# A new order of loads and work at the start of an attention and gMLP block, and six weight loads moved by three blocks

## The chip, the cores and the metric

The kernel runs on one core of one Trainium2 chip. The metric is the device time in microseconds (us) of one execution. Before the change the median was 1889.34 us in 4 runs (1888.5 to 1889.51).

## The reference

```python
mod = (silu(c) @ w_mod).reshape(1, 6, 1, 1024)       # sa, ca, ga, sb, cb, gb
h = layernorm(x) * (1 + ca) + sa                     # x: 2048 rows of 1024
x = x + ga * A(h)      # A: q = h @ wq; 32 heads of 128 against given K and V
                       #    (2048 keys each), softmax, then @ wo
h = layernorm(x) * (1 + cb) + sb
x = x + gb * B(h)      # B: gMLP, 1792 + 1792 columns, 2048 x 2048 spatial product
```

All tensors are bf16. The change touches only the first line of work (the layer norm of x, the modulation with ca and sa, the first query product) and the loads of wq.

## The kernel before

Attention runs in 64 "halves": one head against 1024 of the 2048 queries. Each half has 16 "blocks" kb of 128 keys. A block is two score products ("sps"), one exponential on ACT ("pt"), two output products ("ops"), one DVE addition of the exponentials ("pacc"), and a few products of a later query projection ("qps"), which DVE casts to bf16 ("qT"), as filling. When a half has ended, the sums in pacc go to DRAM and come back transposed ("pT"), DVE reduces them ("den"), and the reciprocals go through DRAM once more ("rec", "rbc"). DVE copies the output products out of PSUM ("ou") and multiplies them by rbc ("oT"). Nearly all loads are issued by one engine, SP, in program order.

```python
    load_wm(nc.scalar, 0, 1)
    load_wm(nc.scalar, 1, 1)
    for j in range(4):                     # SP: x and w_mod interleaved
        for t in range(2):
            nc.sync.dma_start(xg[j][:, t], x_dram[:, 2 * j + t, :])
        load_wm(nc.sync, j, 0)
    ...
    silu()
    for ti in range(9):                    # row tiles 0 to 7 (the first 1024 rows)
        if ti < 8:
            row[ti] = row_stats(xg[ti // 2][:, ti % 2, :])       # DVE
        if ti == 0:
            silu_end()
        else:
            xt = xg[(ti - 1) // 2][:, (ti - 1) % 2, :]
            centre(xt, row.pop(ti - 1), xt)                      # DVE
            if ti % 2 == 0:                # two tiles: turn on PE, copy out on ACT
                ...                        # 16 transposes into hps
                nc.scalar.activation(h1T[...], hps[...], ACT.Copy)
                if j > 0:
                    mod_products(j - 1)    # PE: the columns of ca and sa
                keep_busy(6)               # six dummy matmuls
            elif ti > 3:
                mod_columns(ti // 2 - 2)
    mod_products(3)
    mod_columns(2)
    for j in range(4):                     # h1T = h1T * (1 + ca) + sa
        if j == 3:
            mod_columns(3)
        modulate(2 * j, 0)
        modulate(2 * j + 1, 0, nc.scalar if j else nc.vector)
    keep_busy(8)
    ...
    load_wq(0)                             # 1 MB: the query weights of four heads
    load_kv(0)
    load_wq(1)
    ...
    for g, (i, kb) in enumerate(steps):    # attention: half i, block kb
        ...
        if kb == 2 and i < 16:
            load_kv(halves[i + 1][0])
            if i == 12:
                load_wq(2)
        elif kb == 2 and qh == 0 and h + 1 < H:
            load_kv(h + 1)
            if h % 4 == 2 and h + 2 < H:
                load_wq((h + 2) // 4)
        ...
        if i > 0:
            work = {0: store_sums, 3: turn_sums, 10: finish_den, 13: load_rec}.get(kb)
            if work:
                work(i - 1)
```

The six loads of wq_t inside attention fall into halves 12, 20, 28, 36, 44 and 52.

The softmax here doesn't subtract the row's maximum and nothing guards it: scores larger than these inputs give would overflow.

## Time and profile before

| what | before |
|---|---|
| span of the profiled execution | 1887.7 us |
| PE busy | 1855.4 us (98%) |
| first "pt" of attention (end of the start) | 35.76 us |
| the first 63 of 64 halves of attention, from first pt to first pt | 1119.8 us |
| PE waits for the qT cast ("sps") | 7.7 us, 11 times |

PE is the bound: it is busy 98% of the span and is 90% of the chain. So time can be won only where PE has nothing to do: in the start, and in stalls of attention.

The waits over the whole span (engine and line, what it waited for, us in total, times, longest):

```profile
DVE den L325 <- DMA pT<-sums_dram: 14.9, 8, 3.0
...
PE sps L282 <- DVE qT L266: 7.7, 11, 1.6
...
PE ops L461 <- DVE ou L467: 3.6, 3, 1.7
...
PE qps L262 <- DVE qT L266: 2.6, 3, 1.3
```

Half 12 in the timeline (start, duration, engine, line, what; in brackets the idle time before, and what ended it). A half of this kind takes 17.3 us; this one took 18.98.

```profile
256.19 0.36 SPq L314 DMA_DIRECT2D sums_dram<-pacc  x1
...
256.65 2.16 SPq L244 DMA_TRANSPOSE kT<-in_A_k_cache_dram  x1
...
258.91 0.52 SPq L246 DMA_DIRECT2D v_sb<-in_A_v_cache_dram  x1
...
259.49 1.96 SPq L239 DMA_DIRECT2D wq_t<-in_A_wq_dram  x1
...
261.50 2.74 SPq L318 DMA_TRANSPOSE pT<-sums_dram  x1
...
269.50 1.22 DVE L325 TENSOR_REDUCE den<-pT 128x8 f32<-128x1024 bf16 x1 [2.98 <-DMA pT<-sums_dram]
...
272.43 0.38 PE L282 MATMUL sps<-qT,kT 128*128 128x512 bf16 x1 [1.62 <-DVE qT L266]
```

Read it downwards. The sums are stored at 256.19. Then K, V and 1 MB of wq_t are put into the queue, and only then pT. pT lands at 269.50; DVE has idled 2.98 us for it and, working in order, has left everything behind it undone, also the cast of qT that PE needs. So PE stands 1.62 us.

The start, from the same view:

```profile
18.99 1.28 DVE L126 BATCH_NORM_STATS2 stats<-xg 128x6 f32<-128x512 bf16 x2 [0.17 <-DMA xg<-in_A_x_dram]
...
23.69 1.23 DVE L131 TENSOR_SCALAR xg<-xg,mv,rstd 128x1024 bf16<-128x1024 bf16 x1 [0.31 <-POOL rstd L120]
...
26.53 1.88 ACT L215 ACTIVATE h1T<-hps 128x2048 bf16<-128x2048 bf16 x1 [2.77 <-PE hps L213]
...
28.44 1.92 DVE L195 TENSOR_SCALAR h1T<-h1T,cols 128x1024 bf16<-128x1024 bf16 x4 [0.91 <-ACT h1T L215]
...
30.95 3.62 PE L262 MATMUL qps<-h1T,wq_t 128*128 128x512 bf16 x16
...
34.60 0.69 DVE L266 CAST qT<-qps 128x512 bf16<-128x512 f32 x1 [1.03 <-PE qps L262]
...
35.76 2.85 ACT L450 ACTIVATE pt<-sps 128x1024 bf16<-128x1024 f32 x3 [3.82 <-PE sps L282]
```

The last row tiles of x land at 18.99 (DVE waited 0.17 us), DVE centres the last at 23.69 to 24.92, PE turns it, ACT copies it out of PSUM from 26.53 to 28.41, then DVE and ACT modulate, and the 16 query products run from 30.95. Attention begins with pt at 35.76.

### The profile page before, as it was taken

Reading aid. Unit: us, or ns where it says so; the run is one execution under the profiler, and the core shown is the slowest. Engines: PE = TensorE matmul, PEld = TensorE weight load, DVE = VectorE, ACT = ScalarE, POOL = GpSimd, SP = SyncE. Lnnn points to the kernel's source line nnn. Section 1 sums busy time; section 2 is a strip of 40 time slices with the busy share of each in tenths; the row PEclk is TensorE's granted clock in tenths of the full one; section 3 lists DMA queues with packets and bytes.
Section 4 is the critical chain, followed back from the end, with each engine's and each line's share of the span. In section 5 each row is a group of like instructions: output and inputs, shape, how many; then the busy total and the mean of one; then the engine's idle time right before and its main releaser. Section 6 shows DMA issues by size and latency. Waiting matters only on the chain.

```text
span 1887.7 us, 24331 instructions
## 1 busy us (share of the span) xinstructions
PE 1855.4 (98%) x8873; PEld 851.2 (45%) x8873; DVE 1283.2 (68%) x2131; ACT 1099.4 (58%) x1155; POOL 31.8 (2%) x55
## 2 busy tenths in 40 slices
PE   7999999999999999999999999999999999999999
PEld 3444444444444444444444444444445444444444
DVE  6899888888888888888888888454455400333334
ACT  4888989888888899999999997000013332000000
POOL 1000000000000000000000000000000000000000
PEclk9999999999999999999999999999999999999999
DMA  9585575564555443555565444764214022221102
GB/s 240 146 188 136 135 166 131 128 170 115 140 138 136 116 123 97 151 145 130 150 164 125 114 107 111 191 178 119 66 46 95 6 51 78 52 46 50 45 1 78
DMA packets 396793, 217.35 MB, mean 115 GB/s; under 512 B 297856, under 2 KB 354176, under 8 KB 396672
## 3 DMA queue, kind: packets, MB, share of 16 engines
q1 hardware_dynamic: 392512, 213.70, 44.6%
q10 hardware_dynamic: 4160, 2.10, 0.4%
q8 instruction: 69, 1.13, 0.2%
q14 instruction: 52, 0.43, 0.1%
HBM read 124.26 MB, written 43.52 MB: 89 GB/s over the span
## 4 chain that ended last, share of the span: by engine, by line
PE 90%; DMA 4%; DVE 4%; SPq 1%; issue 1%; ACT 0%; DVEq 0%; ACTq 0%
PE sps L282 20%; PE ops L461 20%; PE acc L372 12%; PE gps L598 10%; PE qps L262 10%; PE zps L548 5%; PE bo L619 5%; PE zps L582 5%; DMA pT<-sums_dram 3%; DVE pacc L471 2%; PE mod_ps L413 1%; DVE den L325 1%; SPq L239 1%; DMA xg<-in_A_x_dram 0%; DVE qT L266 0%
## 5 line engine op out<-in xcount | busy, mean ns | idle before, releaser
L450 ACT ACTIVATE pt<-sps 128x1024 bf16<-128x1024 f32 x1024 | 1017.2, 1025 | 121.2 <-PE sps L282 88.7
L471 DVE TENSOR_TENSOR pacc<-pacc,pt 128x1024 bf16<-128x1024 bf16 x896 | 615.0, 686 | 60.6 <-ACT pt L450 1.3
L282 PE MATMUL sps<-qT,kT 128*128 128x512 bf16 x2048 | 610.7, 379 | 8.5 <-DVE qT L266 7.7
L461 PE MATMUL ops<-pt,v_sb 128*128 128x512 bf16 x2048 | 609.4, 379 | 3.9 <-DVE ou L467 3.6
L262 PE MATMUL qps<-h1T,wq_t 128*128 128x512 bf16 x1024 | 344.3, 379 | 2.6 <-DVE qT L266 2.6
L282 PEld LDWEIGHTS <-kT 128*128 128x128 bf16 x2048 | 200.0, 98 | 253.6 <-issue 16.2
L461 PEld LDWEIGHTS <-v_sb 128*128 128x128 bf16 x2048 | 199.9, 98 | 251.5 <-issue 11.1
L372 PE MATMUL acc<-wo_t,ot 128*128 128x512 bf16 x992 | 216.9, 379 | 0.0
L550 ACT ACTIVATE z<-zps 128x448 bf16<-128x448 f32 x64 | 34.8, 543 | 290.3 <-PE zps L548 287.4
L598 PE MATMUL gps<-wsp,z 128*128 128x512 bf16 x896 | 193.9, 379 | 0.0
L601 DVE TENSOR_TENSOR g<-gps,b_bc 128x512 bf16<-128x512 f32 x56 | 38.7, 692 | 222.1 <-PE gps L598 222.1
L262 PEld LDWEIGHTS <-wq_t 128*128 128x128 bf16 x1024 | 100.1, 98 | 120.9
L372 PEld LDWEIGHTS <-ot 128*128 128x128 bf16 x992 | 96.4, 98 | 113.5
L598 PEld LDWEIGHTS <-z 128*128 128x128 bf16 x896 | 87.7, 98 | 105.7
L266 DVE CAST qT<-qps 128x512 bf16<-128x512 f32 x128 | 88.4, 691 | 41.2 <-PE qps L262 41.0
L548 PE MATMUL zps<-z2w,h2T 128*128 128x448 bf16 x512 | 97.3, 352 | 0.0
L619 PE MATMUL bo<-w_out_t,z1T 128*128 128x512 bf16 x448 | 97.2, 379 | 0.0
L582 PE MATMUL zps<-h2T,z1w 128*128 128x512 bf16 x448 | 96.9, 379 | 0.0
L325 DVE TENSOR_REDUCE den<-pT 128x8 f32<-128x1024 bf16 x63 | 74.8, 1187 | 14.9 <-DMA pT<-sums_dram 14.9
L143 DVE COPY h2T<-hps 128x1024 bf16<-128x1024 bf16 x16 | 11.0, 691 | 97.2 <-PE hps L142 97.2
L346 DVE TENSOR_TENSOR oT<-ou,rbc 128x1024 bf16<-128x1024 f32 x62 | 75.6, 1219 | 0.7 <-DMA rbc<-rec_dram 0.7
L548 PEld LDWEIGHTS <-h2T 128*128 128x128 bf16 x512 | 50.0, 98 | 46.5 <-issue 0.2
(74 smaller groups left out, 695.0 us busy)
## 6 DMA issues: line engine op xcount, KB each, us to landing
rbc<-rec_dram SPq DMA_DIRECT2D x64, 512.0 KB
v_sb<-in_A_v_cache_dram SPq DMA_DIRECT2D x40, 512.0 KB
sums_dram<-pacc SPq DMA_DIRECT2D x63, 256.0 KB
oT_dram<-oT SPq DMA_DIRECT2D x62, 256.0 KB
ot<-oT_dram SPq DMA_DIRECT2D x24, 512.0 KB
wq_t<-in_A_wq_dram SPq DMA_DIRECT2D x8, 1024.0 KB
wm_l<-in_w_mod_dram SPq DMA_DIRECT2D x8, 1024.0 KB
wo_t<-in_A_wo_dram SPq DMA_DIRECT2D x8, 1024.0 KB
```

The source lines that it names most:

```text
L262: nc.tensor.matmul(box["ps"][:], wq_t[:, dc, hc:hc + DH], h1T[:, dc, q0:q0 + 512], start=(dc == 0), stop=(dc == KD - 1))
L266: nc.vector.tensor_copy(out=out_t[:, j * 512:(j + 1) * 512], in_=box["ps"][:])
L282: nc.tensor.matmul(sps[:, j * 512:(j + 1) * 512], kts[h][:, kb * P:(kb + 1) * P], qts[(h, qh)][:, j * 512:(j + 1) * 512], start=True, stop ...
L325: nc.vector.tensor_reduce(out=den[:], in_=state[i]["pT"][:], op=ALU.add, axis=mybir.AxisListType.X)
L372: nc.tensor.matmul(accs[ti][:, sl], lhs, wo_t[:, hh, sl], start=(hh == 0), stop=(hh == H - 1))
L450: nc.scalar.activation(pt[:], s_tiles.pop(g)[:], ACT.Exp, scale=SCALE)
L461: nc.tensor.matmul(o_ps[j][:], vs[h][:, kb, :], pt[:, j * 512:(j + 1) * 512], start=(kb == 0), stop=(kb == NKB - 1))
L471: nc.vector.tensor_add(out=pacc[:], in0=pacc[:], in1=pt[:])
L548: nc.tensor.matmul(zps[:], h2T[:, dc, ti * P:(ti + 1) * P], z2w[:, dc, sl], start=(dc == 0), stop=(dc == KD - 1))
L582: nc.tensor.matmul(zps[:], w[:, dc, :], h2T[:, dc, q * 512:(q + 1) * 512], start=(dc == 0), stop=(dc == KD - 1))
L598: nc.tensor.matmul(gps[:], z2[s][:, f * P:(f + 1) * P], wsps[q][:, s, :], start=(s == 0), stop=(s == NT - 1))
L619: nc.tensor.matmul(bo[:], z1T[:, f, ti * P:(ti + 1) * P], w_out_t[:, f, sl], start=(f == 0), stop=(f == NF - 1))
```

## The change

The intent: shorten the start (load x first; give ACT two of the eight row statistics; modulate the last 256 rows straight out of PSUM, with no copy before; request the first head's wq, K and V early; load the exponential's table first) and keep the 1 MB wq_t loads from standing in front of pT. The dummy matmuls fall from 32 to 10. The core of the diff (helpers and renamings cut):

```diff
+    nc.scalar.activation(small.tile([P, 1], FP32, name="warm_e")[:], eps_tile[:], ACT.Exp)
     load_wm(nc.scalar, 0, 1)
     load_wm(nc.scalar, 1, 1)
-    for j in range(4):
-        for t in range(2):
-            nc.sync.dma_start(xg[j][:, t], x_dram[:, 2 * j + t, :])
-        load_wm(nc.sync, j, 0)
+    for ti in range(8):
+        nc.sync.dma_start(xg[ti // 2][:, ti % 2], x_dram[:, ti, :])
+    load_wm(nc.sync, 0, 0)
+    ...                                   # and 1, 2, 3
+    nc.sync.dma_start(wq_g[0][:, :, 0:256], wq_v[:, :, 0:256])
+    nc.sync.dma_start(out=kts[0][:], in_=A_k_cache[0, 0], transpose=True)
+    nc.sync.dma_start(vs[0][:], A_v_cache[0, 0].rearrange("(kb p) d -> p kb d", p=P))
+    nc.sync.dma_start(wq_g[0][:, :, 256:512], wq_v[:, :, 256:512])
...
+    def stats_act(ti):                    # mean and mean square on ACT
+        ...
+        nc.scalar.activation(junk[:], src, ACT.Identity, scale=1.0 / D, accum_out=mv[:, 0:1])
+        nc.scalar.activation(junk[:], src, ACT.Square, scale=D ** -0.5, accum_out=mv[:, 1:2])
...
-    for ti in range(9): ...
+    dve(0); silu_end(); dve(1); norm(0); stats_act(2); dve(3); norm(1); turn(0)
+    keep_busy(4); mod_products(0); finish_act(2); stats_act(5); dve(4); norm(2); norm(3)
+    turn(1); mod_columns(0); keep_busy(4); dve(6); norm(4); finish_act(5); dve(7); norm(5)
+    turn(2); mod_products(1); mod_products(2); norm(6); norm(7); mod_columns(1)
+    turn(3, False); keep_busy(2); mod_products(3); mod_columns(2)    # tile pair 3 stays in PSUM
+    for dc in range(4):
+        modulate(dc, 0, 768)
+    ...                                   # 768 columns from SBUF, 256 straight from PSUM
...
-    load_wq(0)
-    load_kv(0)
-    load_wq(1)
+    nc.sync.dma_start(wq_g[1][:], wq_v[:, :, 512:1024])
...
-            if i == 12:
-                load_wq(2)
...
-            if h % 4 == 2 and h + 2 < H:
-                load_wq((h + 2) // 4)
...
         if i > 0:
+            if kb == 5 and (i == 12 or i > 16 and qh == 0 and h % 4 == 2 and h + 2 < H):
+                load_wq((h + 2) // 4 if i > 16 else 2)
             work = {0: store_sums, 3: turn_sums, 10: finish_den, 13: load_rec}.get(kb)
```

More of the change, by code (lines that the diff above doesn't have):

```diff
@@ L105, in load_wm @@
         eng.dma_start(wms[j][:, k], wmod_v[:, :, k * D + j * 256:k * D + (j + 1) * 256])
+    wq_v = A_wq.rearrange("(dc p) hd -> p dc hd", p=P)
+    wq_g, kts, vs, qts = {}, {}, {}, {}
+    for g in range(2):
+        wq_g[g] = att.tile([P, KD, 4 * DH], BF16, name="wq_t", tag="wq_t", bufs=2)
+    kts[0] = att.tile([P, S], BF16, name="kT", tag="kT", bufs=2)
+    vs[0] = att.tile([P, NKB, DH], BF16, name="v_sb", tag="v_sb", bufs=2)
+    nc.scalar.activation(small.tile([P, 1], FP32, name="warm_e")[:], eps_tile[:], ACT.Exp)
     load_wm(nc.scalar, 0, 1)
     load_wm(nc.scalar, 1, 1)
-    for j in range(4):
-        for t in range(2):
-            nc.sync.dma_start(xg[j][:, t], x_dram[:, 2 * j + t, :])
-        load_wm(nc.sync, j, 0)
+    for ti in range(8):
+        nc.sync.dma_start(xg[ti // 2][:, ti % 2], x_dram[:, ti, :])
+    load_wm(nc.sync, 0, 0)
+    load_wm(nc.sync, 1, 0)
+    load_wm(nc.sync, 2, 0)
+    load_wm(nc.sync, 3, 0)
+    nc.sync.dma_start(wq_g[0][:, :, 0:256], wq_v[:, :, 0:256])
+    nc.sync.dma_start(out=kts[0][:], in_=A_k_cache[0, 0], transpose=True)
+    nc.sync.dma_start(vs[0][:], A_v_cache[0, 0].rearrange("(kb p) d -> p kb d", p=P))
+    nc.sync.dma_start(wq_g[0][:, :, 256:512], wq_v[:, :, 256:512])
     def ln_stats(chunks):
@@ L168, in keep_busy @@
     def keep_busy(n):
-        zps = bank_ps("zps", [P, 512])
+        zps = side_ps("zps", [P, 512])
         for _ in range(n):
@@ L175, in mod_products @@
     def mod_products(j):
-        mps = mpss[j] = side_ps("mps", [P, 2, 2])
+        mps = mpss[j] = bank_ps("mps", [P, 2, 2])
         for k in range(2):
@@ L187, in mod_columns, with modulate @@
                                     scalar1=1.0)
-    def modulate(dc, t0, eng=nc.vector):
-        sl = h1T[:, dc, t0:t0 + 1024]
+    def modulate(dc, t0, n, eng=nc.vector, src=None):
+        dst = h1T[:, dc, t0:t0 + n]
+        if src is None:
+            src = dst
+        else:
+            dst = dst.rearrange("p (t k) -> p t k", k=P)
         if eng is nc.scalar:
-            nc.scalar.activation(sl, sl, ACT.Identity, bias=cols[:, 0, dc:dc + 1],
+            nc.scalar.activation(dst, src, ACT.Identity, bias=cols[:, 0, dc:dc + 1],
@@ L193, in modulate @@
                                  scale=cols[:, 1, dc:dc + 1])
             return
-        nc.vector.tensor_scalar(out=sl, in0=sl, scalar1=cols[:, 1, dc:dc + 1],
+        nc.vector.tensor_scalar(out=dst, in0=src, scalar1=cols[:, 1, dc:dc + 1],
                                 scalar2=cols[:, 0, dc:dc + 1], op0=ALU.mult, op1=ALU.add)
-    row = {}
-    silu()
-    for ti in range(9):
-        if ti < 8:
-            row[ti] = row_stats(xg[ti // 2][:, ti % 2, :])
-        if ti == 0:
-            silu_end()
-        else:
-            xt = xg[(ti - 1) // 2][:, (ti - 1) % 2, :]
-            centre(xt, row.pop(ti - 1), xt)
-            if ti % 2 == 0:
-                j = ti // 2 - 1
-                hps = wide_ps("hps", [P, 2, KD, P], BF16)
-                for t in range(2):
-                    for dc in range(KD):
-                        nc.tensor.transpose(hps[:, t, dc, :],
-                                            xg[j][:, t, dc * P:(dc + 1) * P], identity[:])
-                nc.scalar.activation(
-                    h1T[:, :, j * 256:(j + 1) * 256].rearrange("p d (t k) -> p d t k", t=2),
-                    hps[:].rearrange("p t d k -> p d t k"), ACT.Copy)
-                if j > 0:
-                    mod_products(j - 1)
-                keep_busy(6)
-            elif ti > 3:
-                mod_columns(ti // 2 - 2)
@@ new lines, with norm @@
+    row, junk = {}, early.tile([P, D], BF16, name="junk")
+    def stats_act(ti):
+        mv = early.tile([P, 2], FP32, name=f"mv{ti}")
+        src = xg[ti // 2][:, ti % 2, :]
+        nc.scalar.activation(junk[:], src, ACT.Identity, scale=1.0 / D, accum_out=mv[:, 0:1])
+        nc.scalar.activation(junk[:], src, ACT.Square, scale=D ** -0.5, accum_out=mv[:, 1:2])
+        row[ti] = (mv, None)
+    def norm(ti):
+        mv, rstd = row.pop(ti)
+        x_t = xg[ti // 2][:, ti % 2, :]
+        centre(x_t, (mv, rstd), x_t)
@@ new lines, in finish_act @@
+    def finish_act(ti):
+        mv = row[ti][0]
+        var = small.tile([P, 1], FP32, name="var", tag="var")
+        nc.vector.scalar_tensor_tensor(out=var[:], in0=mv[:, 0:1], scalar=mv[:, 0:1],
+                                       in1=mv[:, 1:2], op0=ALU.mult, op1=ALU.subtract)
+        nc.vector.tensor_scalar(out=var[:], in0=var[:], scalar1=-1.0, scalar2=EPS,
+                                op0=ALU.mult, op1=ALU.add)
+        rstd = small.tile([P, 1], FP32, name="rstd", tag="rstd")
+        nc.gpsimd.tensor_tensor(out=rstd[:], in0=var[:], in1=neg_half[:], op=ALU.pow)
+        row[ti] = (mv, rstd)
@@ new lines, with turn, dve @@
+    turned_x = {}
+    def turn(j, evacuate=True):
+        hps = turned_x[j] = wide_ps("hps", [P, KD, 2, P], BF16)
+        for t in range(2):
+            for dc in range(KD):
+                nc.tensor.transpose(hps[:, dc, t, :],
+                                    xg[j][:, t, dc * P:(dc + 1) * P], identity[:])
+        if evacuate:
+            nc.scalar.activation(
+                h1T[:, :, j * 256:(j + 1) * 256],
+                hps[:].rearrange("p d t k -> p d (t k)"), ACT.Copy)
+    def dve(ti):
+        row[ti] = row_stats(xg[ti // 2][:, ti % 2, :])
@@ new lines, in turn_k, with out @@
+    def turn_k(j, evacuate=True):
+        k_ps = bank_ps("k_ps", [P, 8, DH], BF16)
+        for kb in range(8):
+            nc.tensor.transpose(k_ps[:, kb, :], k0[:, 8 * j + kb, :], identity[:])
+        def out():
+            nc.scalar.activation(kts[0][:, 1024 * j:1024 * (j + 1)],
+                                 k_ps[:].rearrange("p j d -> p (j d)"), ACT.Copy)
+        if evacuate:
+            out()
+        return out
+    silu()
+    dve(0)
+    silu_end()
+    dve(1)
+    norm(0)
+    stats_act(2)
@@ L223 @@
+    dve(3)
+    norm(1)
+    turn(0)
+    keep_busy(4)
+    mod_products(0)
+    finish_act(2)
+    stats_act(5)
+    dve(4)
+    norm(2)
+    norm(3)
+    turn(1)
+    mod_columns(0)
+    keep_busy(4)
+    dve(6)
+    norm(4)
+    finish_act(5)
+    dve(7)
+    norm(5)
+    turn(2)
+    mod_products(1)
+    mod_products(2)
+    norm(6)
+    norm(7)
+    mod_columns(1)
+    turn(3, False)
+    keep_busy(2)
     mod_products(3)
     mod_columns(2)
-    for j in range(4):
-        if j == 3:
-            mod_columns(3)
-        modulate(2 * j, 0)
-        modulate(2 * j + 1, 0, nc.scalar if j else nc.vector)
@@ L230 @@
-    keep_busy(8)
-    wq_v = A_wq.rearrange("(dc p) hd -> p dc hd", p=P)
+    for dc in range(4):
+        modulate(dc, 0, 768)
+    for dc in (4, 5):
+        modulate(dc, 0, 768)
+        modulate(dc, 768, 256, nc.scalar, turned_x[3][:, dc, :, :])
+    mod_columns(3)
+    modulate(6, 0, 768)
+    modulate(7, 0, 768, nc.scalar)
+    for dc in range(4):
+        modulate(dc, 768, 256, nc.vector, turned_x[3][:, dc, :, :])
+    for dc in (6, 7):
+        modulate(dc, 768, 256, nc.scalar, turned_x[3][:, dc, :, :])
@@ L233 @@
     wo_v = A_wo.rearrange("(h p) n -> p h n", p=P)
-    wq_g = {}
-    kts, vs, qts = {}, {}, {}
     def load_wq(g):
@@ L395, in late_rows @@
         elif 100 <= g < 108:
-            modulate(g - 100, 1024)
+            modulate(g - 100, 1024, 1024)
     def load_row(ti):
```

## The prediction

> **What bounds the kernel now.** The page shows PE busy 1855.4 of 1887.7 us (98%), clock 0.999; the chain of waits is 90% PE. Time can come only from places where PE is not fed: the start, and a few stalls in attention.
>
> *Start.* In the timeline the first "pt" exponential of attention starts at 35.76 us and the first "ops" matmul at 37.91. Before that: DMA (the last xg lands at 18.97), DVE statistics (about 2.08 us per row tile with centring, eight tiles, to 24.9), transposes, a 1.88 us ACT copy (to 28.41), modulation (ACT to 31.95), 16 query matmuls (to 34.57), the qT cast (to 35.29). DMA moves about 320 GB/s until 24 us (stage table).
>
> *Wq stalls.* In the waits, DVE "den" waits for pT 14.9 us over 8 times. Six of these (near 266, 410, 556, 699, 838, 977 us) follow a 1 MB wq_t load, which sits between the sums' store and their transposing load in one in-order queue; pT then takes 6.2 to 8.0 us in the chain. "den" blocks DVE, the qT cast comes late, and PE's "sps" waits 1.6, 0.3, 1.1, 0.7, about 0, 0.8 us: together about 4.5 us.
>
> **What the change does.**
> 1. wq_t loads move from block 2 to block 5 of a half, behind the pT load. The six pT waits should vanish: **-4.5 us**, all on the path, because PE is the bound there. The 1 MB then competes with the reciprocals' store and load (blocks 10 and 13), 5 blocks of about 1.1 us later; I expect no new wait. Two early stalls without a wq load (PE "ops" waits 1.71 us near 75 and 132) stay.
> 2. Start: statistics of tiles 2 and 5 move to ACT (two activations of about 1.17 us each, against 1.6 us of DVE per tile); the last 256 columns are modulated straight from PSUM, which takes one 1.88 us copy off the path; all xg loads come before SP's wm loads; wq, K and V are requested earlier. The exp table load (1.28 us) goes before ACT's DMA issues.
>    But the bytes before attention hardly change: x and wm are 6.3 MB, at 320 GB/s 20 us, so the last wm still lands near 22 us, and wm0 only near 16. DVE waits in program order for cols(0), and finish_act(2) waits for ACT, whose last wm issue holds it until about 10.5. So DVE's saving (2.5 us) is partly lost; my step-by-step sum puts the last qT cast near 32.3 us, against 35.29: **-3 us** (1 to 5). K should land near 28.5, V near 30.5: in time.
>    Fewer dummy matmuls (10, against 32) may leave the clock at half during the query products; the Trainium skill ("TensorE: Matmul & The Clock Gate", the HAM clock gate) says that an idle window of about 3.4 us halves it. Here the granted clock was 0.50 from 24 to 26 us, and dummy 512-column matmuls took about 0.46 us each near 13 us, 0.24 near 18. I count up to 1.5 us for it.
>
> The rest (steady attention, projections, gMLP) keeps its instructions.
>
> **Prediction.** 1889.3 - 4.5 - 3.3 = about 1881.5 us; 1877.5 to 1885.5 should hold it 8 times in 10. Faster by over 2%: 1%; within 2%: 98%; slower by over 2%: 1%.
>
> **What would show it.** Right: "den" waits for pT only about twice (2 us), the six PE waits gone; first "pt" near 32.5 us. Wrong: new waits of "oT" for rbc after a wq load; first "pt" at 35 or later because of wm, kT or v landing, ACT order or a half clock; or below 30 if the loads come faster.
>
> **What would make it wrong.** Attention's early stage (DVE 90% busy) may absorb or amplify a shifted DMA schedule; clock phase; when wm lands.

## More of the kernel before

From the page: the span, the first busy line, the line of the instruction queue (packets, megabytes, share of 16 DMA engines) and the chain that ended last.

```profile
span 1887.7 us, 24331 instructions
...
PE 1855.4 (98%) x8873; PEld 851.2 (45%) x8873; DVE 1283.2 (68%) x2131; ACT 1099.4 (58%) x1155; POOL 31.8 (2%) x55
...
q8 instruction: 69, 1.13, 0.2%
...
PE 90%; DMA 4%; DVE 4%; SPq 1%; issue 1%; ACT 0%; DVEq 0%; ACTq 0%
```

## The result, and the profile after

The changed kernel takes 1878.56 us (median of 9 runs, 1877.75 to 1879.23), 10.5 us less. The ratio is 0.9944, 95% interval 0.9935 to 0.9954. The two profiled spans differ by 11.4 us: the profiled execution of the kernel before (1889.51) was 0.5 us above the median, that of the changed kernel (1878.07) 0.5 us below.

```profile
span 1876.3 us, 24304 instructions
...
PE 1849.9 (99%) x8851; PEld 849.7 (45%) x8851; DVE 1283.1 (68%) x2133; ACT 1100.5 (59%) x1165; POOL 31.7 (2%) x55
...
q8 instruction: 69, 1.13, 0.3%
...
PE 92%; DVE 4%; DMA 1%; SPq 1%; issue 1%; ACT 1%; POOL 0%; DVEq 0%; ACTq 0%; POOLq 0%
```

In the chain DMA has fallen from 4% to 1%. The waits:

```profile
PE qps L342 <- DVE qT L346: 3.3, 3, 1.4
...
PE ops L535 <- DVE ou L541: 2.9, 2, 1.7
...
PE sps L362 <- DVE qT L346: 2.5, 5, 1.2
...
DVE den L403 <- DMA pT<-sums_dram: 1.9, 2, 1.0
...
DVE stats L139 <- DMA xt<-in_A_x_dram: 1.6, 1, 1.6
```

The waits of den for pT are 1.9 us in place of 14.9. Half 12 again: pT is now issued at 252.97 in front of wq_t at 256.34, den (260.20) shows no wait, and PE none either.

```profile
249.97 0.36 SPq L392 DMA_DIRECT2D sums_dram<-pacc  x1
...
250.43 1.87 SPq L324 DMA_TRANSPOSE kT<-in_A_k_cache_dram  x1
...
252.39 0.53 SPq L326 DMA_DIRECT2D v_sb<-in_A_v_cache_dram  x1
...
252.97 2.70 SPq L396 DMA_TRANSPOSE pT<-sums_dram  x1
...
256.34 0.43 SPq L319 DMA_DIRECT2D wq_t<-in_A_wq_dram  x1
...
260.20 1.18 DVE L403 TENSOR_REDUCE den<-pT 128x8 f32<-128x1024 bf16 x1
```

The start:

```profile
12.92 0.22 DVE L232 SCALAR_TENSOR_TENSOR var<-mv 128x1 f32<-128x1 f32 x1 [1.02 <-ACT junk L221]
...
14.78 0.93 PEld L193 LDWEIGHTS <-wm 128*128 128x128 bf16 x32 [0.99 <-DMA wm<-in_w_mod_dram]
...
23.25 2.43 DVE L212 TENSOR_SCALAR h1T<-h1T,cols 128x768 bf16<-128x768 bf16 x6
...
23.83 1.02 ACT L209 ACTIVATE h1T<-hps,cols 128x256 bf16<-128x256 bf16 x2 [0.62 <-PE hps L246]
...
25.63 3.63 PE L342 MATMUL qps<-h1T,wq_t 128*128 128x512 bf16 x16 [0.63 <-DMA wq_t<-in_A_wq_dram]
...
29.30 0.69 DVE L346 CAST qT<-qps 128x512 bf16<-128x512 f32 x1 [1.03 <-PE qps L342]
...
30.45 2.85 ACT L524 ACTIVATE pt<-sps 128x1024 bf16<-128x1024 f32 x3 [1.79 <-PE sps L362]
```

DVE waits 1.02 us for ACT's statistics, and PE waits for the first w_mod until 14.78; but the modulation begins at 23.25, not 28.44, and the query products start at 25.63, as soon as the first half of wq has landed. The first pt comes at 30.45.

One new wait, just behind the start. The first xt (a tile of 128 rows from the second half of x) lands late; DVE stands 1.57 us for it, the qT cast behind it is late, and PE stands 1.36 us:

```profile
36.99 1.29 DVE L139 BATCH_NORM_STATS2 stats<-xt 128x6 f32<-128x512 bf16 x2 [1.57 <-DMA xt<-in_A_x_dram]
...
39.96 0.38 PE L342 MATMUL qps<-h1T,wq_t 128*128 128x512 bf16 x1 [1.36 <-DVE qT L346]
```

To see where time went, both traces were cut at the first pt of each half. The column "change" is the difference of that part:

```
part                                   before     after    change
start (to the first pt)                 35.76     30.45     -5.31
half 0                                  17.42     18.86     +1.44
halves 1 to 3                           55.58     55.52     -0.06
halves 4, 5, 6                          58.56     56.26     -2.30
halves 12/13, 20/21, 28/29, 36/37,
  44/45, 52/53 (the wq_t halves)                            -5.47
all other halves                                             0.00
from half 63 to the end                732.10    732.36     +0.26
span                                   1887.7    1876.3    -11.4
```

The terms of the start and of the wq_t halves had been expected, at least in sign; two had not: the loss in half 0 and the gain in halves 4 to 6.

### The profile page after: what moved, and what is told of

The parts are those of the page before. It is cut to its first block, busy times and chain, and to the rows that moved or that the text cites. A ratio compares the mean times of both kernels' runs of the same rounds, so it can differ in the third digit from the quotient of the medians. Undisturbed runs are those within 1.5% of the kernel's fastest.

```text
span 1876.3 us, 24304 instructions
## 1 busy us (share of the span) xinstructions
PE 1849.9 (99%) x8851; PEld 849.7 (45%) x8851; DVE 1283.1 (68%) x2133; ACT 1100.5 (59%) x1165; POOL 31.7 (2%) x55
## 4 chain that ended last, share of the span: by engine, by line
PE 92%; DVE 4%; DMA 1%; SPq 1%; issue 1%; ACT 1%; POOL 0%; DVEq 0%; ACTq 0%; POOLq 0%
PE sps L362 21%; PE ops L535 21%; PE acc L450 12%; PE qps L342 11%; PE gps L674 10%; PE zps L624 5%; PE bo L695 5%; PE zps L658 5%; DVE pacc L545 2%; PE mod_ps L491 1%; ACT pt L524 1%; DMA xt<-in_A_x_dram 0%; PE hps L155 0%; DMA xg<-in_A_x_dram 0%; DVE den L403 0%
```

## The experiments

Theory at the outset: the change is two independent parts. The wq_t part removes the six pT stalls; the start part brings attention forward, less what half 0 gives back. For halves 4 to 6 there were two theories. Theory F: PE's instruction fetches share the DMA engines with the transposing loads, and 22 fewer dummy matmuls shift where they fall. Rival S: the earlier start or the new load order made these halves shorter. Twelve kernels were run; all gave right results. "h4-6" below is the sum of halves 4, 5 and 6, and "wq" is the length of the twelve wq_t halves above that of the same halves where no stall occurs, both from the single profiled run.

```
kernel        median us (runs)  beside before  ratio    first pt  half 0   h4-6    wq   PE dummies
before          1889.02 (13)                              35.76    17.42   58.56  5.47   32
after           1878.56  (9)      1889.02      0.9944     30.45    18.86   56.26  0.01   10
wq_only         1883.30  (4)      1888.21      0.9975     34.80    17.42   58.62  0.00   32
start_only      1886.53  (4)      1888.21      0.9991     30.95    18.64   56.24  9.26   10
pad22           1880.62  (4)      1888.21      0.9962     32.59    17.96   57.10  0.00   32
wq1_late        1877.65  (4)      1888.21      0.9945     30.79    17.42   56.23  0.00   10
before_less     1890.20  (4)      1888.53      1.0006     35.51    17.42   56.58  8.25   10
pad_h           1879.38  (4)      1888.53      0.9950     31.18    18.54   57.01  0.00   32
stats_dve       1881.27  (4)      1888.53      0.9959     34.49    17.42   56.23  0.01   10
copy3           1881.01  (4)      1888.53      0.9959     33.31    17.42   56.60  0.00   10
after_again     1878.20  (5)      1888.89      0.9947     30.87    18.11   56.23  0.00   10
best            1878.77  (5)      1888.89      0.9950     31.35    18.18   56.23  0.00   10
wm_between      1883.26  (4)      1888.89      0.9971     36.83    17.42   56.23  0.00   10
wq_whole        1880.81  (4)      1888.89      0.9959     33.41    17.42   56.23  0.00   10
```

### wq_only: the wq_t part alone

```diff
 # on the kernel before
-            if i == 12:
-                load_wq(2)
...
-            if h % 4 == 2 and h + 2 < H:
-                load_wq((h + 2) // 4)
+            if kb == 5 and (i == 12 or i > 16 and qh == 0 and h % 4 == 2 and h + 2 < H):
+                load_wq((h + 2) // 4 if i > 16 else 2)
```

> The kernel before, with only the later six wq_t loads moved from block 2 to block 5. Theory (the stalls are pT queued behind 1 MB of wq_t): the waits of den for pT fall from 8 to 2, halves 12, 20, 28, 36, 44 and 52 become as short as their neighbours of the same kind, and nothing else moves: the changed kernel's share there is 5.5 us, so about 1883.5 us, with the first pt still near 35.8 us and halves 4 to 6 as before (19.3, 19.5, 19.8 us). Rival (the start's new DMA schedule did it): the waits stay and the time is about 1889.

Measured: 1883.30 us against 1888.21, ratio 0.9975 (0.996 to 0.999). The wq_t halves lose all of their 5.47 us, and halves 4 to 6 stay at 58.62. The waits of den fall from 14.9 to 2.0 us, in 3 waits and not 2. Its start was 1 us shorter than in the other profile of the same start (the first pt at 34.80 in place of 35.76). This part of the theory holds by itself: a 1 MB load in front of pT was the stall.

### start_only: the start part alone

```diff
 # on the changed kernel
+            if i == 12:
+                load_wq(2)
...                       # and the others; all six back to block 2
-            if kb == 5 and (i == 12 or i > 16 and ...):
-                load_wq((h + 2) // 4 if i > 16 else 2)
```

> The changed kernel with the six wq_t loads put back to block 2. Theory (two independent parts): first pt near 30.5, half 0 at 18.9, halves 4 to 6 near 18.8, 18.9, 18.6, and the six wq waits of 5.5 us back: about 1884 us. Rival (the parts interact): the six halves are no longer than their neighbours, about 1878.6, or the sum of both parts differs from the whole by over 1.5 us.

Measured: 1886.53 us, ratio 0.9991 (0.9976 to 1.0005). Start, half 0 and halves 4 to 6 are as expected, but the stalls came back as 9.26 us, not 5.5. So the expectation was missed by 2.5 us and the parts do interact: one alone is worth 4.9 us of median, the other 1.7, together 6.6, while the whole is worth 10.5. (The profiled execution of start_only took 1887.46 us, 0.9 above the median of its four, so the 9.26 us are those of one of the longer executions.) Half 20 in start_only shows how a stall grows (timeline; then busy time of the engines, granted clock, DMA share and GB/s by stretch):

```profile
407.26 1.22 DVE L403 TENSOR_REDUCE den<-pT 128x8 f32<-128x1024 bf16 x1 [3.92 <-DMA pT<-sums_dram]
```

```profile
408.00:410.00 2.00, 0.00 (x0) 0.00 (x0) 1.93 (x5) 0.10 (x1) 0.00 (x0) 0.96 0.00 1
410.00:412.00 2.00, 1.80 (x5) 0.70 (x5) 1.79 (x4) 1.02 (x1) 0.00 (x0) 0.50 0.01 2
412.00:414.00 2.00, 2.00 (x8) 0.76 (x7) 1.38 (x3) 1.02 (x1) 0.00 (x0) 0.69 0.71 236
```

DVE waits 3.92 us for pT, PE is idle for the whole stretch from 408 to 410 us (its longest wait for the qT cast is 2.6 us), and then the granted clock is 0.50: from 409.8 us the throttle has cut it for one period of 3.4 us. Half 20 lost 2.84 us and half 21 another 1.35. The Trainium skill ("TensorE: Matmul & The Clock Gate", What's actually happening) gives the idle window that halves the clock as about 3.4 us and calls it free-running; here a wait of 2.6 us was followed by one such period, while the waits of up to 1.62 us at wq_t loads in the kernel before were not. The last section counts the work of PE in such windows.

### pad22: as many PE instructions as before

```diff
 # on the changed kernel
     silu()
+    zpad = side_ps("zpad", [P, 512])
+    for _ in range(22):
+        nc.tensor.matmul(zpad[:, 0:8], zeros[:, 0:P], zeros[:, 0:8], start=True, stop=True)
     dve(0)
```

> The changed kernel with 22 tiny dummy matmuls (8 columns) while PE waits at the start, so that PE has exactly as many instructions as before. Theory F (halves 4 to 6 gained 2.3 us because PE's instruction fetches, one 16 KB packet per 256 PE instructions, no longer fall into the transposing loads of K): the fetches fall back to the old places relative to the half, halves 4 to 6 are 19.3, 19.5, 19.8 us again, about 1880.9 us. Rival S (halves 4 to 6 gained because attention starts earlier or because the DMAs' semaphore lanes shifted): they stay at 18.8, 18.9, 18.6 and the time at 1878.6.

Measured: 1880.62 us, but for a mixed reason. h4-6 rose from 56.26 to 57.10, not to 58.6: a third of the effect. And the start was 2 us longer, because this time the granted clock was 0.50 from 22.2 to 29.0 us and the query products took 4.76 us, not 3.63. The runs spread over 1879.2 to 1882.09. So the median agrees with theory F for a wrong reason; the test had to be made again without touching the start.

### before_less: the kernel before with 10 dummy matmuls

```diff
 # on the kernel before
-                keep_busy(6)
+                keep_busy(2)
...
-    keep_busy(8)
+    keep_busy(2)
```

> The kernel before with 10 dummy matmuls at the start in place of 32, as many PE instructions as the changed kernel; start work, loads and wq order as before. Theory F (PE's instruction fetch phase sets halves 4 to 6 and the size of the wq stalls): halves 4, 5, 6 become 18.8, 18.9, 18.6 us (sum 56.2, not 58.6), and the six wq halves lose more than before's 5.5 us, nearer the 8.9 us of the start-only run. Rival S (the new start's load order sets them): sum stays at 58.6 and the wq stalls at 5.5 us. For the start: without dummies the clock may be at half during the query products: first pt 35 to 38 us.

Measured: h4-6 fell from 58.6 to 56.58 and the wq stalls rose to 8.25 us, with the old load order and the old start (the 8.9 us quoted for start_only was a first count; counted as in the table above it is 9.26). Rival S falls for 2.0 of the 2.3 us: neither the new loads nor an earlier start (35.51) is needed. As the two effects nearly cancel, the time is 1890.20 us, ratio 1.0006 (0.9991 to 1.0021). The granted clock fell here too after half 20's stall (a wait of PE of 2.1 us; 0.50 from 414.2 us on for 3.4 us). The waits that go with the term are den for pT in half 4 and oT for rbc in half 6. The first two lines are of the kernel before, the other two of the changed kernel:

```profile
124.69 1.22 DVE L325 TENSOR_REDUCE den<-pT 128x8 f32<-128x1024 bf16 x1 [1.00 <-DMA pT<-sums_dram]
...
154.37 1.22 DVE L346 TENSOR_TENSOR oT<-ou,rbc 128x1024 bf16<-128x1024 f32 x1 [0.75 <-DMA rbc<-rec_dram]
```

```profile
119.70 1.18 DVE L403 TENSOR_REDUCE den<-pT 128x8 f32<-128x1024 bf16 x1
...
148.15 1.22 DVE L424 TENSOR_TENSOR oT<-ou,rbc 128x1024 bf16<-128x1024 f32 x1
```

The DMA records of the traces show where the 16 KB packets of the q8 queue ("fetch") fall, in us from the start of the half, beside these waits and the lengths of the halves. The two padded kernels, pad22 above and pad_h below, are in the table too:

```
profiled   PE       half 4:               half 5:   half 6:
kernel     dummies  fetch  den    length  length    fetch  oT     length
                    at     waits                    at     waits
before        32      9.3   1.00   19.28   19.51      4.9   0.75   19.77
wq_only       32      9.3   0.81   19.09   19.51      5.1   1.00   20.03
pad_h         32      9.6   0.65   18.92   19.51      3.6   0.00   18.58
pad22         32      9.3   0.25   18.80   19.24      4.1   0.38   19.05
before_less   10     15.6   0.00   18.78   18.87      7.7   0.00   18.93
after         10     15.0   0.00   18.80   18.88      7.5   0.00   18.58
start_only    10     14.8   0.00   18.79   18.87      8.0   0.00   18.58
```

The kernels with 32 dummies have issued 44 PE instructions more, so the packet comes earlier in the half, in this table by 5.2 us or more in half 4 and by 2.4 or more in half 6. At 9.3 us it falls into the transposing load of K; in the profile of the kernel before, K's packets of 256 bytes take 76 ns on average in the microsecond of the fetch and about 19 ns in the one before, only 17 of them start in the next microsecond (in most others of this half's transposing loads 750 to 1000 packets of this size do), and pT, queued behind, lands late enough for DVE to wait 1.0 us. The other profiles agree: in half 4 the first 2048 packets of 256 bytes, as many as K has, start within 3.5 to 3.9 us in the four kernels with 32 dummies and within 1.9 to 2.1 us in all ten with 10. Half 4 grows by what den waits beyond about 0.5 us; half 5, which holds no such packet, is longer only where den waited in half 4. A part of half 6 is something else: before_less keeps 18.93 us there, and copy3 below, with 10 dummies, has 18.94. That is the 0.3 us that before_less leaves.

### pad_h: the padding, with the start left alone

```diff
 # on the changed kernel, in emit_s
         sps = wide_ps("sps")
+        if 2 <= g < 24:
+            nc.tensor.matmul(sps[:, 0:8], zeros[:, 0:P], zeros[:, 0:8], start=True, stop=True)
         for j in range(2):
```

> The changed kernel with 22 tiny dummy matmuls (8 columns, into the score tile before its real product overwrites it) spread over halves 0 and 1, so that PE has as many instructions as before from half 2 on and the start is untouched. Theory F: first pt 30.5 to 31, halves 4 to 6 sum 57.5 to 58.6 us in place of 56.2, at least 1.3 us of the 2.3 back. Rival S: the sum stays at 56.2. Either way halves 0 and 1 may be up to 1 us longer.

Measured: h4-6 is 57.01 us. That is between the two expectations: half 5 is back at the 19.51 us of the kernel before, half 4 is 18.92, half 6 has not changed (18.58). The time is 1879.38 us. So adding the instructions to the changed kernel brings back 0.75 us of 2.3 here and 0.84 in pad22; taking them out of the kernel before takes out 2.0. The number of PE instructions is a cause of this term: strong one way, weak the other, and halves 1 to 3 vary by more between profiles (54.87 to 56.45 us) than the padding brings back. The table above shows why the term did not come back whole. The padding did not put the packets quite where they had been: in half 6 they fall at 3.6 (pad_h) and 4.1 us (pad22), not at 4.9 to 5.1, and oT waits 0.00 and 0.38 us, not 0.75 to 1.00. In half 4 they fall at 9.3 to 9.6 us again, but den waits only 0.65 and 0.25 us, most of which costs nothing there. Why the packet delays K by these different amounts was not found.

### wq1_late: the second wq_t load out of the way of xt

```diff
 # on the changed kernel
-    nc.sync.dma_start(wq_g[1][:], wq_v[:, :, 512:1024])
...
+        if g == 5:
+            nc.sync.dma_start(wq_g[1][:], wq_v[:, :, 512:1024])
```

> The changed kernel with the load of wq_t 1 (1 MB, used first in half 3) issued in block 5 of half 0 in place of before the first xt. Theory (half 0 is 1.44 us longer than before because xt lands late behind that 1 MB, so stats, then the qT cast, then PE are late): no wait of stats for xt, half 0 near 17.4 us, about 1877.2 us. Rival (xt is late because of K, V and the second wq half): half 0 stays near 18.9 and the time at 1878.6.

Measured: half 0 is 17.42 us, as in the kernel before, and there is no wait for xt. The mechanism is right. The gain is not settled: the first pt came 0.34 us later in this profile and half 1 was 0.17 us longer, so 1.0 us is left in the span, and the ratio, 0.9945, is that of the changed kernel (0.9944 and 0.9947).

### stats_dve, copy3, wm_between, wq_whole: parts of the start undone

```diff
 # stats_dve, on the changed kernel
-    stats_act(2)
+    dve(2)
...
-    finish_act(2)
-    stats_act(5)
...
-    finish_act(5)
+    dve(5)
```

```diff
 # copy3, on the changed kernel
-    turn(3, False)
+    turn(3)
...
-        modulate(dc, 0, 768)
-        modulate(dc, 768, 256, nc.scalar, turned_x[3][:, dc, :, :])
...
+    for dc in range(6):
+        modulate(dc, 0, 1024, nc.scalar if dc in (3, 5) else nc.vector)
+    mod_columns(3)
+    modulate(6, 0, 1024)
+    modulate(7, 0, 1024, nc.scalar)
```

```diff
 # wm_between, on the changed kernel
-    for ti in range(8):
-        nc.sync.dma_start(xg[ti // 2][:, ti % 2], x_dram[:, ti, :])
-    load_wm(nc.sync, 0, 0)
...
+    for j in range(4):
+        for t in range(2):
+            nc.sync.dma_start(xg[j][:, t], x_dram[:, 2 * j + t, :])
+        load_wm(nc.sync, j, 0)
```

```diff
 # wq_whole, on the changed kernel
-    nc.sync.dma_start(wq_g[0][:, :, 0:256], wq_v[:, :, 0:256])
+    nc.sync.dma_start(wq_g[0][:], wq_v[:, :, 0:512])
...
-    nc.sync.dma_start(wq_g[0][:, :, 256:512], wq_v[:, :, 256:512])
```

> The changed kernel with all eight row statistics on DVE (none on ACT). Theory (ACT's statistics take DVE work off the start's path): DVE does 2 x 1.65 us more and saves 1.0 us of waiting for ACT and 0.7 us of finishing, so the last centring ends 1.5 us later (23.7 in place of 22.2), first pt near 31.5 to 32, about +1.2 us in all. Rival (the start is set by the loads of wm and wq): first pt stays at 30.5 to 30.9.

> The changed kernel with the last 256 columns copied by ACT out of PSUM first and all modulated in 1024 columns, as before. Theory (the direct modulation takes one 1.88 us copy off the path): modulation starts near 25.7 in place of 23.3 and ends near 29.3, first pt near 32.5, +2 us. Rival (wq's landing at 25.6 sets the start of the query products and hides it): first pt 31 at most.

> The changed kernel with the SP loads of x and w_mod interleaved as in the kernel before (two rows of x, one piece of w_mod, and so on). Theory (x first is what lets DVE run without waiting): the statistics of tile 6 wait for x until about 17 and of tile 7 until about 19, the last centring ends about 1 us later than 22.3, first pt near 31.5. Rival (wm, not x, sets the start): wm0 lands by 11 and the first pt is at 30.5 or earlier.

> The changed kernel with the first wq_t loaded as one 1 MB piece before K and V. Theory (the first query product waits for wq's landing, 0.6 us in the changed kernel): 0.5 MB more at about 320 GB/s is 1.6 us, so the products start near 27.2 and the first pt comes near 32.0, 33.5 if the clock falls to half meanwhile. Rival (modulation sets it): 30.5 to 31.

Measured: undone one at a time, each part delays the first pt (30.45 to 30.95 with all of them): wm_between to 36.83, stats_dve to 34.49, wq_whole to 33.41, copy3 to 33.31. The sign was right each time, and two sizes were far too small (wm_between +5.9 or more and not +1, stats_dve +3.5 or more and not +1.2). Part of it is DVE's work: in stats_dve the last centring ended at 24.89, 2.66 us later than in the changed kernel (22.23) and not 1.5. The rest is the clock, here in stats_dve:

```profile
22.00:24.00 2.00, 0.73 (x8) 0.73 (x9) 1.86 (x6) 0.00 (x0) 1.10 (x2) 0.83 1.17 322
24.00:26.00 2.00, 2.00 (x69) 2.00 (x68) 1.11 (x3) 1.67 (x1) 0.61 (x1) 0.50 1.25 265
26.00:28.00 2.00, 2.00 (x17) 1.72 (x17) 1.98 (x7) 0.46 (x2) 0.00 (x0) 0.50 1.04 228
28.00:30.00 2.00, 1.78 (x35) 1.24 (x35) 1.21 (x5) 1.01 (x3) 0.00 (x0) 0.50 0.85 238
```

PE was busy 0.18 us of the 2 us before these lines and 0.73 of the first (it stood idle from 20.2 to 23.3 us); from 23.3 to 30.1 us the clock was 0.50, and turns, products of w_mod and query products all took longer. In wm_between it was 0.50 for 10.2 us, and there DVE waited for x 9.6 us in all (4.2 in the changed kernel):

```profile
DVE stats L137 <- DMA xg<-in_A_x_dram: 9.6, 5, 3.9
```

So x first is the largest single part of the start. Its worth, and that of ACT's statistics, is probably in part that PE is not left without work long enough to lose its clock; this is read from the two profiles and was not isolated. For wq_whole and copy3 the sizes were nearly right (33.41 where 33.5 was expected with a clock at half, 33.31 where 32.5 was). The parts are not additive: together they are worth 5.3 us, and these four differences add up to more than 14. Not all of a delay is lost, either: in all four kernels half 0 is 17.42 us, because attention then starts late enough for xt to be in time. By the medians, the four kernels take 4.7, 2.7, 2.3 and 2.5 us more than the changed kernel.

### after_again and best: a combined version

```diff
 # best, on the changed kernel: wq1_late, and
-    nc.sync.dma_start(wq_g[0][:, :, 0:256], wq_v[:, :, 0:256])
+    nc.sync.dma_start(wq_g[0][:, :, 0:DH], wq_v[:, :, 0:DH])
...
-    nc.sync.dma_start(wq_g[0][:, :, 256:512], wq_v[:, :, 256:512])
+    nc.sync.dma_start(wq_g[0][:, :, DH:512], wq_v[:, :, DH:512])
```

> The changed kernel once more, unaltered, as the partner of the combined version in the same rounds. About 1878.5 us; first pt 30.4 to 31, half 0 near 18.9, halves 4 to 6 sum 56.2 to 56.6, no wq stall.

> The changed kernel with the second wq_t load moved to block 5 of half 0, and the first piece of wq cut from 256 to 128 columns (the one head that the first query products need), so that it lands about 0.6 us earlier. Theory: query products start near 25.0 in place of 25.6, first pt near 30.0, half 0 near 17.4: about 1.5 to 2 us less than the changed kernel of the same rounds, 1876.7 us. Rival (half 0's gain is given back in half 1, or 256-byte pieces are too slow): within 0.5 us of the changed kernel.

Measured: after_again 1878.20 us, ratio 0.9947; best 1878.77, ratio 0.9950. The combined version is not faster. The query products started at 26.47, not 25.0; the clock of this run was at 0.50 from 22.4 to 25.8 us. And the second piece of wq, now 768 KB behind V, was late for the next head's products:

```profile
33.60 0.82 PE L342 MATMUL qps<-h1T,wq_t 128*128 128x512 bf16 x3 [0.58 <-DMA wq_t<-in_A_wq_dram]
```

The unaltered kernel, for its part, lost only 0.69 us in half 0 this time (18.11), where the first profile had lost 1.44; but its half 1 was 0.54 us longer, so that the two halves together lost 1.17 us against 1.38.

## Why the prediction was right or wrong

The time, 1878.56 us, lies inside the predicted 1877.5 to 1885.5, and the gain of 10.5 us is larger than the 7.8 predicted. That the number came so near is partly luck: the two terms that nobody expected, +1.44 us in half 0 and -2.30 in halves 4 to 6, nearly cancel. The mechanisms of the two terms that were predicted are right, and their sizes too small. Point by point:

- *The wq_t stalls: right in mechanism, about a fifth too small.* Predicted 4.5 us, measured 5.47 both in the changed kernel and in wq_only. The 4.5 was the sum of PE's listed "sps" waits only. In half 12 the listed wait is 1.62 us and the two halves lost 1.76.
- *den waits about twice, 2 us: right* (2 waits, 1.9 us), in part by luck: of the two that were to stay, that of half 4 went and one in half 9 came. *No new wait behind the moved load: nearly right.* oT waits for rbc 1.7 us in 3 waits (0.7 in 1 before), and no half is longer for it.
- *The start: too small.* Predicted 3 us for the start itself, measured 5.31 to the first pt. The last qT cast ended at 29.99, not 32.3. Two steps of the sum were too large; what each is worth was not measured. First, "DVE waits in program order for cols(0)" cost nothing: PE's products for it began at 14.78, where w_mod was expected near 16, and the columns were written at 15.83 with no wait of DVE. Second, the "up to 1.5 us" counted for a half clock was not needed: in this profile the clock was full from 20.8 us on. Here the phase of the clock helped the comparison: in the profile of the kernel before it was 0.50 from 22.9 to 26.3 us, in that of wq_only it was not, and against the start of wq_only (34.80) the gain is 4.35 us. The half clock was a real risk: in pad22, pad_h, stats_dve, wm_between, wq_whole, copy3 and best the clock fell in the start, and pad22's query products took 4.76 us in place of 3.63. The table load that goes before ACT's DMA issues delayed little: it ran from 0.73 us, and the issues began beside it at 0.94, where they had begun at 0.73. The wait for ACT's statistics was as predicted: ACT began them at 10.55 us, and DVE waited 1.02 us.
- *K and V in time: right. The 1 MB of the second wq_t load: overlooked.* It stands in front of the first xt and gave back 1.44 us in half 0 (0.69 in the second profile, with 0.54 more in half 1); wq1_late shows the cause.
- *"The rest keeps its instructions": true, and still not enough.* Halves 4 to 6 gained 2.3 us that the prediction did not have. The number of dummy PE instructions at the start decides where PE's instruction fetches fall in later halves: before_less moves these halves by 2.0 us with the loads and the work of the start as they were. That the fetch delays the transposing loads on the DMA engines is the likely link: in half 4 it goes with the slower K load in all 14 profiles. It was not isolated.
- *"Two early stalls without a wq load stay": half right.* Half 2 is the same to 0.01 us; the wait near 132 us shrank from 1.71 to 1.15 us, as part of halves 4 to 6.
- *The two parts add up: wrong, and hidden.* On top of the new start, moving wq_t is worth 9.26 us of stalls, not 5.47. before_less (8.25) shows that fewer dummies with the old start make the stalls nearly as large in sum, though not half by half: half 12 loses nothing there, and 0.6 us in start_only. The clock drop after half 20 is 1.35 us of that in start_only. Why the stalls of start_only also grow in halves 36 and 44, in which no q8 packet falls, stays open.

## What to carry to other kernels

Look at what an in-order queue holds between a store and the load that reads it back, and move large loads that nobody needs soon behind it; then look at what the moved or added load now stands in front of. When a change takes instructions away at one place, compare the stages that it did not touch as well, half by half, because instruction fetches (here the likely link) and the clock can carry its effect there. A kernel that fills PE with dummies needs its start judged over several profiles, since a clock period of 3.4 us at half speed comes and goes between runs.

## What the Trainium skill lacked or had wrong

- "DMA: Bandwidth & Descriptors" (Issuing engines are not separate DMA queues) says that DMAs of scalar, sync and gpsimd run on the same 16 engines and interleave. "Runtime: NRT & Kernel Launch" (Instruction fetch mechanics) says that instructions are fetched in blocks of 16 KiB, 256 at a time, through a DMA queue of the sequencer's own. The traces agree: PE's fetches are 69 packets of 16 KB, one for about 257 PE instructions. What no page gives is what a fetch costs the loads that it meets: here each takes 0.9 to 1.9 us, and their position alone goes with 2.0 us in three halves (before_less).
- "DMA: Bandwidth & Descriptors" (Queues, rings and completion order) says that descriptors of a ring are consumed in order. The traces agree: with 1 MB of wq_t ahead, pT was waited for until 8.0 us after its issue (half 12), and the wait went away when the order was changed. The page has no figure for such a delay.
- "TensorE: Matmul & The Clock Gate" (What's actually happening) names at least one idle window of about 3.4 us as the condition. It does not say how much work a window may hold and still count as idle. Here the clock fell to 0.50 after waits of PE of 2.6 us (start_only) and 2.1 us (before_less). Counted back 3.41 us from the fall, the window held 1.21 and 1.34 us of PE work; all other windows of attention in the 14 profiles, on the same grid, held 1.70 us or more, and none was followed by a fall. In the start it also fell after windows with more (2.02 us in the kernel before, from 19.5 to 22.9 us), so busy time alone does not give the rule. The lengths of the low periods, 3.4, 6.8 and 10.2 us, agree with the page's window.
- "ScalarE: Activation LUTs" does not give the cost of the accumulator output. Here each statistics ACTIVATE of 128x1024 took 1.06 us and was followed by a separate read of the accumulator of 0.19 us.
